# Reversed filter rows through a DRAM scratch and adding transfers: one change to a two-headed kernel (local attention beside a long convolution)

## The chip, the cores and the metric

The kernel runs on one core of a Trainium2 chip. A core has TensorE (PE in the profile, with PEld for its weight loads), VectorE (DVE), ScalarE (ACT), GpSimd (POOL) and SyncE (SP, which here only issues transfers), and 16 DMA engines that all queues share. The metric is the device time of one launch in microseconds, smaller is better: the median of several executions. Beside it stands one execution taken by the profiler, from which every duration below comes.

## The reference

Two independent computations stand side by side in the output (2048 rows, 576 columns each). Everything is bf16 in and out.

```
A: qkv = x @ wqkv; 32 heads of 18; each position attends to 8 positions, 2 apart
   logits = sum(q * k_gathered) * 18**-0.5; softmax over 8; o = sum(attn * v_gathered)
   a = o @ wo
B: k_shift = sum over 4 taps of k shifted by t, times shift_k;  kv = k_shift * v
   kv_f = rfft2(kv padded to (4096, 576));  kf_f = rfft2(ssm_k padded to 4096)
   y = irfft2(kv_f * kf_f)[:2048]  +  kv * ssm_D;   b = q * y
out = concat(a, b)
```

B is a causal convolution of kv with the filter ssm_k along the sequence, channel by channel; adding ssm_D to the filter's first tap gives the second term.

## The kernel before

**Part B** cuts the sequence into four blocks of 512. Each block of the filter (m = 0 to 3) and of kv (i = 0 to 3) is turned into a spectrum of 512 odd frequencies by matmuls against tables of cosines and sines (`filter_spectrum`, units "fk" and the block's number; `x_spectrum`, units "fx"). Output block j is the sum over i of the product of spectrum i of kv with spectrum j - i of the filter (`products`, on DVE, for three column groups t), summed by matmuls against an identity (`sums`, `sum_of`), turned back by matmuls (`inverse`, units "inv") and multiplied by q. A complex product is made with three real ones, so every spectrum has a third part, the sum of the first two: either an addition on DVE (`add_third`, or in `produce`) or, by `third`, a copy on SP's queue and an adding transfer on POOL's. Of the homes that receive products there are two for j = 0 and four for later j; DVE waits for PE before it writes one again.

A filter block stands in SBUF with 512 taps as four chunks of 128 partitions (`kTok`). The table is symmetric, so tap n and tap 512 - n can first be added and subtracted ("folded"), and the matmuls then need half the rows. For this the rows of the first two chunks have to be reversed. `fold_filter` does it on PE: for each half, matmuls against a reversing matrix, one that handles a single first row, and an identity, into PSUM (`ps_rev`), 12 matmuls for blocks 3 and 2 and 8 for blocks 1 and 0, two ACT evacuations, then three adding transfers on POOL. Before that, POOL copies one chunk of each block to a second place (`other`), SP moves the first rows of blocks 0 and 1 in a chain of six small copies (`first_rows`), and DVE negates a row of each block (`negate`).

**Part A** is projected by matmuls (units "proj" and "v", 8 to 18 matmuls each with one evacuation for two units), the logits are products on DVE that PE sums over a head's 18 columns (`logits`, `ps_log`), softmax is spread over DVE, ACT and PE, and the weighted sum over v is again products on DVE and sums on PE (`weigh`, `ps_acc`), then `output` (units "wo").

**The order** is written out by hand. DVE's work runs through the program in a fixed order: the taps (blocks 0 to 3), ten products of `logits(0)`, ten of `logits(1)` with softmax between, then `weigh` with n from 1 to 26, then `products`. PE's pieces that DVE does not wait for at once stand in one queue, `units`. At each call of `until()` the next number in `PLACES` says how many pieces are taken from its front and issued. The first four numbers belong to the taps, the fifth stands ahead of the logits, the next five behind every second product of `logits(0)`, then softmax and `logits(1)`, and so on. `need(label)` takes from the front until no piece with that label is left. `FKS` and `FXS` mix the spectra with the v projections; `EARLY` puts the first fk3 pieces between the last two mirrors (pieces labelled "x" that fold kv); `ZMIX`, `PRE`, `REGROUP` and `AT` place steps of the products, adds of thirds, the regrouping of v's weights, and the mirrors. Every engine works through its own list in order and waits by semaphores, so a piece that isn't ready stops those behind it on its engine.

**Queues.** SP issues the loads, the four transposing loads of the filter (`load_filter`), then `first_rows`, then much later the spreading of the attention weights and the copies of `third`. POOL issues all adding transfers and some loads (`load_q`, which fetch q for part B into `TB`).

Of the kernel before, what the change touches and what calls it, by code (L numbers as in the profile page):

```python
# [19 lines left out]
    2, 1, 1, 0, 1, 4,  # L20
# [3 lines left out]
    25, 22,  # L24
)

THIRDS = ((0, 1),), ((0, 2), (1, 2)), ((0, 3), (1, 3))

REGROUP = (
    15, 14,  # L30
# [3 lines left out]
    2, 14, 13, 4, 3, 0, 2, 4, 8, 2, 10, 2, 6, 1, 4, 4, 3, 6, 1, 3, 0, 5, 5, 5, 3, 3, 4, 2, 1, 0, 3, 11, 2, 2, 3,  # L34
    1, 1, 4, 0, 10, 0, 3, 0, 2, 11, 1, 1, 0,
# [10 lines left out]
    0, 0, 2,  # L46
# [3 lines left out]
    1, 5, 19,  # L50
# [9 lines left out]
def kernel(  # L60
# [40 lines left out]
    GORD = [0, 2, 1, 3]  # L101
    HD = 288
# [163 lines left out]
    flip1 = main.tile([128, 128], BF16, name="flip1")  # L266
    flip0 = main.tile([128, 128], BF16, name="flip0")
    corner = main.tile([128, 128], BF16, name="corner")
    corner2 = main.tile([128, 128], BF16, name="corner2")
    flip2r = main.tile([128, 128], BF16, name="flip2r")  # L270
    identn0 = main.tile([128, 128], BF16, name="identn0")
# [28 lines left out]
    nc.gpsimd.affine_select(flip1[:], ones128[:], pattern=[[1, 128]], compare_op=ALU.is_equal, fill=0.0,  # L300
                            base=-128, channel_multiplier=1)
    nc.gpsimd.tensor_copy(flip0[:], flip1[:])
    nc.gpsimd.tensor_copy(flip2r[:], flip1[:])
    nc.gpsimd.memset(flip1[0:1, 0:1], 1.0)
    nc.gpsimd.memset(flip2r[0:1, 0:1], 2.0 ** 0.5)
    nc.gpsimd.memset(corner[:], 0.0)
    nc.gpsimd.memset(corner2[:], 0.0)
    nc.gpsimd.memset(corner2[0:1, 0:1], 2.0 ** 0.5)
    nc.gpsimd.memset(corner[0:1, 0:1], 1.0)
    nc.gpsimd.tensor_copy(identn0[:], identn[:])  # L310
    nc.gpsimd.memset(identn0[0:1, 0:1], 0.0)
    nc.gpsimd.tensor_scalar(ident2[:], ident[:], 2.0, None, op0=ALU.mult)
# [241 lines left out]
    def with_sine(f, n):  # L554
        f()
        sines[n]()
        if n == 1:
            nc.gpsimd.memset(TK[0:1, 0, 1, :], 0.5)
            for gi, sg in enumerate((1, -1, -1, 1)):
                nc.gpsimd.memset(TK[0:1, 0, 0, 128 * gi:128 * gi + 128], sg * 0.5)  # L560
# [69 lines left out]
    logits_run = [False]  # L630

# [6 lines left out]
    def first_rows():  # L638
        nc.gpsimd.dma_start(row(0, 0), B_ssm_D.unsqueeze(0), accum_op=ALU.add)
# [8 lines left out]

    def spare(m):
        return view(Ks, k_at(1, 0) + D * m, [[1, D]])[0:1]  # L650

    signed = set()

    def negate(*ms):
# [691 lines left out]
```

## Time and profile before

| | us |
|---|---|
| median of 3 executions | 212.2 (212.09 to 212.56) |
| profiled execution | 212.5 |
| its span in the trace | 210.8 |

In the profile a line of a timeline gives start, duration, engine, source line, operation, output <- input, how many were merged, and in brackets the idle time before it with what ended that. Groups give a total and the mean of one in ns. Matmuls overlap in PE's pipeline, so for their cost the chain of waits (which counts each once) is the better row. The granted clock of PE is at 1.00 in nearly all of the span.

### The profile page before, as it was taken

How to read it: one execution, taken by the hardware profiler on the slowest of the kernel's cores; microseconds unless marked ns; L12 is line 12 of the kernel's file. 1: busy time of each engine (PE TensorE's matmuls, PEld its weight loads, DVE VectorE, ACT ScalarE, POOL GpSimd, SP SyncE). 2: the span in 40 equal slices, each digit the busy share in tenths (PEclk: the TensorE clock that was granted, in tenths of full speed). 3: DMA queues.
4: the chain of work that ended last, by engine and by line, in shares of the span. 5: the costliest groups of instructions: out<-in, count | busy, mean ns of one | idle time of the engine just before them, and what ended most of it. 6: DMA issues, size and time to landing. Idle time of an engine off the chain costs nothing.

```text
span 210.8 us, 5106 instructions
## 1 busy us (share of the span) xinstructions
PE 200.1 (95%) x2114; PEld 110.7 (53%) x2122; DVE 193.1 (92%) x146; ACT 150.5 (71%) x218; POOL 74.0 (35%) x111
## 2 busy tenths in 40 slices
PE   7999999999999999899999999999989999999891
PEld 2443443344554656564354666656555666666460
DVE  7989999999999999858889999999999849999981
ACT  3799988657684989986369788855666796775540
POOL 8999993001195516320175000002029004033000
PEclk9999999999999999999999999999999999999999
DMA  6999998999639336999999997587559995985133
GB/s 201 303 328 231 266 342 280 170 192 182 151 75 122 48 40 87 180 181 171 235 225 238 194 234 159 105 208 185 153 223 255 239 322 110 214 243 182 28 113 111
DMA packets 35396, 39.66 MB, mean 188 GB/s; under 512 B 17619, under 2 KB 29007, under 8 KB 35374
## 3 DMA queue, kind: packets, MB, share of 16 engines
q1 hardware_dynamic: 26812, 24.88, 47.2%
q0 software_dynamic: 6096, 11.96, 30.4%
q10 hardware_dynamic: 2466, 2.51, 3.5%
q8 instruction: 16, 0.26, 0.5%
q14 instruction: 6, 0.05, 0.1%
HBM read 13.11 MB, written 4.72 MB: 85 GB/s over the span
## 4 chain that ended last, share of the span: by engine, by line
PE 80%; ACT 10%; DVE 5%; issue 2%; DVEq 0%; ACTq 0%
PE ps_proj L378 16%; PE ps_z L1126 9%; PE ps_wo L1029 8%; PE ps_acc L973 7%; PE ps_inv L1158 7%; PE ps_fx L776 6%; PE ps_log L847 4%; PE ps_proj L500 3%; PE ps_fk L627 3%; PE ps_proj L382 3%; PE ps_proj L389 3%; ACT Ks L695 3%; PE ps_rev L673 2%; PE ps_fk L628 1%; ACT qk L977 1%
## 5 line engine op out<-in xcount | busy, mean ns | idle before, releaser
L378 PE MATMUL ps_proj<-xw 128*128 128x512 bf16 x153 | 37.4, 380 | 0.6 <-issue 0.3
L832 DVE TENSOR_TENSOR av<-qk 128x4096 bf16<-128x4096 bf16 (+1 forms) x16 | 31.7, 2013 | 2.8 <-PE ps_log L847 2.8
L378 PEld LDWEIGHTS <-xw 128*128 128x128 bf16 x160 | 14.0, 97 | 20.5 <-issue 6.2
L1099 DVE TENSOR_TENSOR qk<-xw,Ks 128x2304 bf16<-128x2304 bf16 x14 | 18.5, 1355 | 2.5 <-PE ps_inv L1158 2.4
L1139 ACT ACTIVATE av<-ps_z 128x768 bf16<-128x768 f32 x20 | 15.3, 808 | 6.2 <-PE ps_z L1126 6.2
L414 ACT ACTIVATE qk<-ps_proj 128x1024 bf16<-128x1024 f32 x14 | 14.3, 1023 | 7.6 <-PE ps_proj L389 3.3
L695 ACT ACTIVATE Ks<-ps_fk 128x576 bf16<-128x576 f32 x32 | 18.6, 717 | 1.3 <-PE ps_fk L628 1.3
L577 DVE TENSOR_TENSOR tB<-kj,skb 128x4608 bf16<-128x4608 bf16 (+1 forms) x8 | 19.3, 2417 | 0.1
L778 ACT ACTIVATE xw<-ps_fx 128x576 bf16<-128x576 f32 x32 | 18.4, 666 | 0.0
L776 PE MATMUL ps_fx<-xw,TB 128*128 128x288 bf16 x128 | 18.0, 286 | 0.2
L1055 POOL DMA_DIRECT2D Ks<-Ks x3 | 3.7, 1218 | 41.1 <-PE ps_wo L1029 28.7
L1029 PE MATMUL ps_wo<-qk 128*128 128x288 bf16 x128 | 17.8, 287 | 0.0
L627 PE MATMUL ps_fk<-Ks,TB 128*128 128x384 bf16 x62 | 16.9, 326 | 0.8 <-ACT Ks L695 0.7
L414 ACT ACTIVATE v<-ps_proj 128x1024 bf16<-128x1024 f32 x9 | 9.3, 1029 | 9.3 <-PE ps_proj L378 4.3
L973 PE MATMUL ps_acc<-av,ident 64*64 64x512 bf16 x160 | 15.3, 377 | 0.0
L628 PE MATMUL ps_fk<-Ks,TB 128*128 128x192 bf16 x62 | 15.2, 245 | 0.0
L776 PEld LDWEIGHTS <-TB 128*128 128x128 bf16 x128 | 12.0, 97 | 6.0 <-issue 2.9
L1029 PEld LDWEIGHTS <-qk 128*128 128x128 bf16 x128 | 11.6, 98 | 5.6 <-issue 3.0
L1158 PE MATMUL ps_inv<-av,TI 128*128 128x288 bf16 (+1 forms) x96 | 13.6, 293 | 0.6 <-ACT av L1139 0.6
L1161 ACT ACTIVATE v<-ps_inv 128x576 bf16<-128x576 f32 (+1 forms) x14 | 9.5, 677 | 6.3 <-PE ps_inv L1158 6.3
L977 ACT ACTIVATE qk<-ps_acc 128x1024 bf16<-128x1024 f32 x8 | 8.2, 1024 | 8.0 <-PE ps_acc L973 8.0
L956 DVE TENSOR_TENSOR av<-Ks,v 128x4096 bf16<-128x4096 bf16 x6 | 13.6, 2286 | 0.2 <-PE ps_acc L973 0.2
(199 smaller groups left out, 471.3 us busy)
## 6 DMA issues: line engine op xcount, KB each, us to landing
Ks<-Ks POOLq DMA_DIRECT2D x9, 576.0 KB, 7.1
TB<-av SPq DMA_DIRECT2D x12, 256.0 KB, 5.5
kj<-in_B_k_dram SPq DMA_DIRECT2D x6, 504.0 KB, 6.1
vt<-in_B_v_dram SPq DMA_DIRECT2D x8, 288.0 KB, 5.2
Ks<-av SPq DMA_DIRECT2D x8, 256.0 KB, 5.5
Ks<-Ks SPq DMA_DIRECT2D x3, 576.0 KB, 6.1
Ks<-in_A_x_dram SPq DMA_DIRECT2D x2, 576.0 KB, 5.2
xw<-in_A_wqkv_dram SPq DMA_DIRECT2D x2, 576.0 KB, 5.9
```

The costliest lines, as they stand in the source:

```text
L378: nc.tensor.matmul(ps[:, jp, :], wq(kb, comp, 128 * ct, 128), xT(kb, 1024 * jj + 512 * jp, 512), **se)
L414: nc.scalar.activation(view(t, o + pad + 1024 * jj, [[512, 2], [1, 512]]), ps[:], ACT.Copy)
L577: dve(2304 * n, lambda: nc.vector.tensor_tensor(to, view(kj, row * D, [[D, n], [D, 4], [1, D]]), view(skb, row * D, [[D, n], [0, 4], [1, D ...
L627: nc.tensor.matmul(o[:, 0:2], w, rhs[:, 0:2], start=start, stop=stop)
L695: nc.scalar.activation(view(Ks, k_at(m, cs ^ (m & 1)) + 96 * gi, [[768, 3], [384, 2], [1, 96]]), acc3(ps), ACT.Copy, scale=(PSG, MSG)[cs][ ...
L776: nc.tensor.matmul(ps[:, pm, 0:HD], TX[:, 2 * pm + c, 128 * gi:128 * gi + 128], kv[:, 2 * c + pm, HD * h:HD * h + HD], start=(c == 0), sto ...
L832: return P, at, step, dve(1024 * nj, lambda: nc.vector.tensor_tensor(view(P, at, [[step, 4], [256, nj], [1, 256]]), view(t, o + 256 * hh, ...
L973: nc.tensor.matmul(acc[64 * o:64 * o + 64, h, :], ident[64 * h:64 * h + 64, 64 * h:64 * h + 64], view(P, 256 * u, [[2048, 2], [1, 256]])[6 ...
L1029: nc.tensor.matmul(ps[:, r, 0:HD], oT(hh, 2 * c + r, t)[:, o:o + 128], wo[:, t // 2, t % 2, HD * h:HD * h + HD], start=(t == 0 and h == 0) ...
L1099: r = dve(3 * QTR, lambda: nc.vector.tensor_tensor(pr, view(xw, HB * XG[i] + QTR * t, [[HB, 3], [1, QTR]]), view(Ks, k_at(j - i, 0) + QTR ...
L1126: nc.tensor.matmul(view(acc[r], 512 * h, [[192, 2], [96, 2], [1, 96]])[o:o + 64], w[64 * h:64 * h + 64, 64 * h:64 * h + 64], pr[64 * h:64 ...
L1158: nc.tensor.matmul(ps[:, c, 0:n], TI[:, sl, pm, 128 * c:128 * c + 128], Y(j, pm)[:, sl, c0:c0 + n], start=(pm == 0 and sl == 0), stop=(sl ...
```

## The change

The reversal of blocks 2, 1 and 0 leaves PE. `turn_rows` writes the first two chunks of such a block to a scratch in DRAM (`bounce`, 130 rows of two chunks) with the row order reversed, on SP's queue: two large writes and three single rows for each block, in place of `first_rows`. `fold_filter` then has ACT write the negated and scaled base (four activations: `other`, two chunks, one row), and four adding transfers on POOL's queue add the reversed rows from DRAM to all four chunks and to `other`, by half the partitions at a time. The signs and the weight of the first row come from per-partition scales (`keep`, `minus`) and from a table row set to `KAPPA` instead of 0.5. Block 3 is still reversed by matmuls; its `other` is now written by ACT. POOL's four copies and DVE's `negate` go.

The rest concerns order. Folds 2, 1 and 0 enter the queue at places 2, 5 and 9 (`FOLDS`); six fk3 pieces are early, now behind both mirrors. The third part of block 0 of both spectra is left to `produce`, in three pieces; block 1 of kv (at n = 21) takes the place of block 1 of the filter among the thirds by transfer. Thirds of block 2 are issued ahead of `load_q`. Products of output blocks 2 and 3 have six homes instead of four, a home still in use is passed over, and output pieces of the first half of the heads ("wo0") must be issued before. All tables of the order have new numbers.

```diff
 ZMIX = (
-    2, 1, 1, 0, 1, 4,
+    3, 1, 0, 0, 1, 5,
 PRE = (
-    25, 22,
+    27, 33,
-THIRDS = ((0, 1),), ((0, 2), (1, 2)), ((0, 3), (1, 3))
+THIRDS = ((0, 0), (0, 1), (1, 1)), ((0, 2), (1, 2)), ((0, 3), (1, 3))
+BY_DMA = (
+    37, 32, 21,
 REGROUP = (
-    15, 14,
+    0, 7,
 PLACES = (
-    2, 14, 13, 4, 3, 0, 2, 4, 8, 2, 10, 2, 6, 1, 4, 4, 3, 6, 1, 3, 0, 5, 5, 5, 3, 3, 4, 2, 1, 0, 3, 11, 2, 2, 3,
-    1, 1, 4, 0, 10, 0, 3, 0, 2, 11, 1, 1, 0,
+    6, 11, 13, 5, 1, 1, 3, 4, 11, 3, 9, 3, 3, 1, 2, 5, 3, 4, 0, 5, 0, 5, 5, 6, 2, 5, 4, 1, 2, 1, 2, 12, 2, 2, 3,
+    1, 0, 5, 1, 2, 0, 3, 1, 9, 12, 1, 1, 0, 2, 11, 0, 0,
 FKS = (
-    5, 1, 0, 0, 0, 0, 0, 0, 0, 0, 0, 0, 0, 0, 0, 3, 0, 0, 0, 0, 0, 0, 0, 0, 0, 0, 0, 0, 0, 0,
+    5, 1, 0, 0, 0, 0, 0, 0, 0, 0, 0, 0, 0, 0, 0, 0, 0, 0, 0, 2, 0, 0, 0, 0, 0, 1, 0, 0, 2, 0,
 FXS = (
-    0, 0, 15, 0, 8, 0, 0, 4, 0,
+    0, 1, 1, 25, 2, 0, 0, 0, 0,
+FOLDS = (
+    2, 5, 9,
 EARLY = (
-    0, 0, 2,
+    0, 0, 6,
 AT = (
-    1, 5, 19,
+    0, 8, 9,
...
+    bounce = [dram.tile([130, 2 * D], BF16, name=f"bounce{m}") for m in range(NBL)]
...
-    def first_rows():
-        nc.gpsimd.dma_start(row(0, 0), B_ssm_D.unsqueeze(0), accum_op=ALU.add)
-        for step in range(3):
-            for m in (1, 0):
-                nc.sync.dma_start(*((spare(m), row(m, 0)), (row(m, 0), row(m, 1)), (row(m, 1), spare(m)))[step])
...
+    def turn_rows(m):
+
+        kt, t = kTok(m), bounce[m]
+        for c in range(2):
+            nc.sync.dma_start(bass.AP(tensor=t.tensor, offset=t.offset + 64 * 2 * D + (1 - c) * D,
+                                      ap=[[65 * 2 * D, 2], [-2 * D, 64], [1, D]]), kt[:, c, :])
+        nc.sync.dma_start(bass.AP(tensor=t.tensor, offset=t.offset + 65 * 2 * D, ap=[[2 * D, 1], [1, 2 * D]]),
+                          kTok(m)[0:1, 0:2, :].rearrange("p c d -> p (c d)"))
+        for c in range(2):
+            nc.sync.dma_start(bass.AP(tensor=t.tensor, offset=t.offset + (1 - c) * D, ap=[[2 * D, 1], [1, D]]),
+                              kt[64:65, c, :])
...
         def unit():
...
+            t = bounce[m]
+            act = nc.scalar.activation
+            act(other(m), kt[:, 2, :], ACT.Copy, scale=keep[:])
+            act(kt[:, 0, :], kt[:, 2, :], ACT.Copy, scale=minus[:])
+            act(kt[:, 1, :], kt[:, 3, :], ACT.Copy, scale=-1.0)
+            act(row(m, 2), row(m, 2), ACT.Copy, scale=1.0 / KAPPA)
+            clk["A"] += 2.5
+            for h in range(2):
+                rows = t.offset + 65 * 2 * D * (1 - h)
+                p = slice(64 * h, 64 * h + 64)
+                nc.gpsimd.dma_start(view(Ks[p], k_at(m, 2), [[2 * D, 2], [1, 2 * D]]),
+                                    bass.AP(tensor=t.tensor, offset=rows, ap=[[2 * D, 64], [0, 2], [1, 2 * D]]),
+                                    accum_op=ALU.add, max_dma_last_dim=4 * D)
+                nc.gpsimd.dma_start(other(m)[p], bass.AP(tensor=t.tensor, offset=rows, ap=[[2 * D, 64], [1, D]]),
+                                    accum_op=ALU.add)
+
+        def by_matmuls():
...
-            for m in (3, 2, 1, 0):
-                nc.gpsimd.dma_start(other(m), kTok(m)[:, 2, :])
-            first_rows()
+            nc.gpsimd.dma_start(row(0, 0), B_ssm_D.unsqueeze(0), accum_op=ALU.add)
+            for m in (2, 1, 0):
+                turn_rows(m)
...
-            now, first = first[0] + [fold_filter(2)] + first[1] + mirrors[:1] + first[2] + mirrors[1:], list(now)
+            now, first = first[0] + mirrors[:1] + first[1] + mirrors[1:] + first[2], list(now)
...
+    for m, at in zip((2, 1, 0), FOLDS):
+        units.insert(min(at, [u[2] for u in units].index(f"fk{m}")), fold_filter(m))
...
-        npr[0] = npr[0] + 1 if t < 2 or j else 0
+        if j > 1:
+            homes += ((qk, 0), (qk, HB))
+        if j > 1:
+            need("wo0")
+        while homes[npr[0] % len(homes)] in busy.values():
+            npr[0] += 1
+        home = busy[j, t, i] = homes[npr[0] % len(homes)]
+        npr[0] += 1
...
+            if new and (j, t) == (NBL - 1, 2):
+                until()
...
-            for x, m in THIRDS[0]:
+        for at, (x, m) in zip(BY_DMA, THIRDS[0]):
+            if n == at:
                 third(x, m)
...
     outputs(1, 1)
+    for x, n in THIRDS[1]:
+        third(x, n)
     load_q(0)
     load_q(1)
-    for x, n in THIRDS[1]:
-        if x:
-            need(f"fx{n}")
-        third(x, n)
...
```

More of the change, by code (lines that the diff above doesn't have):

```diff
@@ L1077, in store_b @@
     def store_b(j, c0, n, src, h):
-        other = nc.scalar if j == NBL - 1 else nc.sync
+        end = j == NBL - 1
+        other = nc.scalar if end else nc.sync
         if h == 0:
```

86 lines of the change are left out of this document (38 added, 48 removed).

## The prediction

> **What bounds the kernel now.** First the page's head and busy times, then the table of stages:
>
> ```profile
> span 210.8 us, 5106 instructions
> ...
> PE 200.1 (95%) x2114; PEld 110.7 (53%) x2122; DVE 193.1 (92%) x146; ACT 150.5 (71%) x218; POOL 74.0 (35%) x111
> ...
> 50.00:60.00 10.00, 9.37 (x88) 5.37 (x86) 9.90 (x10) 7.56 (x13) 3.11 (x6) 1.00 0.67 152
> 60.00:70.00 10.00, 9.95 (x101) 4.74 (x98) 10.00 (x8) 6.46 (x11) 6.24 (x8) 1.00 0.68 91
> 70.00:80.00 10.00, 9.91 (x98) 5.85 (x91) 9.96 (x7) 9.07 (x16) 4.96 (x6) 1.00 0.35 47
> 80.00:90.00 10.00, 9.24 (x80) 5.75 (x82) 8.82 (x7) 10.00 (x17) 4.63 (x5) 1.00 0.90 146
> ...
> 160.00:170.00 10.00, 10.00 (x136) 6.34 (x135) 7.78 (x7) 7.98 (x13) 3.12 (x4) 1.00 1.07 259
> 170.00:180.00 10.00, 10.00 (x147) 6.76 (x145) 8.41 (x7) 7.65 (x13) 2.34 (x2) 1.00 0.76 211
> ...
> 190.00:200.00 10.00, 9.09 (x179) 5.81 (x168) 10.00 (x9) 5.57 (x8) 1.92 (x3) 1.00 0.34 100
> 200.00:211.00 11.00, 5.76 (x88) 3.67 (x80) 5.53 (x7) 2.60 (x4) 0.00 (x0) 0.95 0.38 107
> ```
>
> The columns are busy times of PE, PEld, DVE, ACT and POOL, then granted clock, DMA share and GB/s. PE is full nearly throughout. Its work is a queue of pieces that only has to be finished, so the end moves by the PE work taken out plus the PE idle time put in or removed. DVE is as full from 50 to 80 us. ACT is full from 80 to 90, where PE loses 0.76 us. In the tail (190 on) DVE is at 100% and PE loses 0.91 us to 200 and, up to its end at 206.2, 6.2 - 5.76 = 0.4 us more: 1.3 us.
>
> **PE work removed.** The chain of waits and the groups show a reversal:
>
> ```profile
> 68.38 0.98 PE ps_rev L673 x8
> ...
> L676 ACT ACTIVATE Ks<-ps_rev 128x576 bf16<-128x576 f32 x8 | 4.8, 648 | 2.1 <-PE ps_rev L673 2.1
> ...
> 71.13 4.47 ACT L695 ACTIVATE Ks<-ps_fk 128x576 bf16<-128x576 f32 x8
> ...
> 93.14 1.71 ACT L695 ACTIVATE Ks<-ps_fk 128x576 bf16<-128x576 f32 x3
> ```
>
> Eight matmuls take 0.98 us, 0.1225 each. Block 2 had 12, blocks 1 and 0 had 8 each; block 3 keeps its 12. So 28 x 0.1225 = **3.4 us of PE** go, and six activations with them.
>
> **ACT work added.** Each of the three folds now has four activations of 576 columns in place of two, and block 3's fold has two more: 12 + 2 - 6 = 8 more. No row has one from SBUF to SBUF of this size; the nearest are the evacuations above, 0.648 us alone and 4.47 / 8 = 0.56 us in a series. A one-row activation with 576 columns is taken at the same price; bounds 8 x 0.56 = 4.5 us and 8 x 0.648 = 5.2. I take 4.5, since they stand in series. ACT's idle time from 60 to 80 us is 3.54 + 0.93 = 4.5 us by the table above, so they just fit if they come early enough; if the cover is gone, up to 5.2 us come onto the ACT-bound stretch from 80 us. The queue count below pops fold 2, 1 and 0 at the logits' second, third and fourth pair, about 61 to 70 us, where that idle time lies. I take **0**, bounds 0 and +4.5.
>
> The Trainium skill, "ScalarE: Activation LUTs", section "What ACT_TABLE_LOAD costs", says that each [128,1] pointer operand adds about 93 ns; seven of the new activations have such a scale, an estimate of 0.65 us on top. No activation with a pointer as its scale is in the trace to test this.
>
> **The order of PE's queue, by hand.** Popping counts ahead of the first logits were 3, 0, 2, 4, 8, 2; now 1, 1, 3, 4, 11, 3. The queue began v24, v24, v00, v00, fx, fk3; now both mirrors are popped by the "x" label and the six early fk3 stay ahead of everything: fk3, fk3, fold2, fk3, fk3, fold1, fk3, fk3, v24, fold0, v24, fx, v00, v00, fk3, fx, fk3, then fk2. The rows that price it:
>
> ```profile
> 50.61 0.61 PE ps_fold L606 x8
> ...
> 55.01 0.41 PE L673 MATMUL ps_rev<-Ks,identn 128*128 128x288 bf16 x2
> ...
> 55.02 1.75 DVE L901 TENSOR_SCALAR xw<-Ks 128x1152 int32<-128x1152 int32 x2
> ...
> 56.70 4.47 DVE L832 TENSOR_TENSOR av<-qk 128x4096 bf16<-128x4096 bf16 x2
> ...
> 59.73 1.92 PE L382 MATMUL ps_proj<-xw 128*64 128x512 bf16 x16
> ...
> 62.89 1.05 PE L847 MATMUL ps_log<-av,E 128*32 128x512 bf16 x16
> ...
> 63.87 3.40 DVE L832 TENSOR_TENSOR av<-qk 128x4096 bf16<-128x4096 bf16 x2
> ```
>
> Before, PE had fold 2 and three v pieces ahead of the first logits and came late: products ready at 61.17, logits at 62.89. Now the second of L901's two copies (0.58 us) and two sign changes (0.43) are no longer ahead of the products, so they are ready at about 60.2. PE by then has only the mirrors and two fk3 and is done at about 59.6 (estimate: fold 3 ends at 55.3, its last row less the pipeline's overlap, mirrors two times 0.61, fk3 two times 0.5, and waits for their evacuations): idle 0.6. Second pair: products every 2.2 us, ready at 64.6; PE has two fk3 (1.0) and half the logits: idle 1.9. Third pair: two fk3 and a v piece against DVE until 68.0 (a half product, 3.40 less 2.2, and a whole one): idle 0.4. From the fourth pair (11 pieces, 6.7 us) PE is behind DVE again. Sum 2.9, less about 0.3 us of waits there before: **+2.6 us of PE idle**, bounds 0 (PE never ahead of DVE) and 4.0 (three gaps with no piece at all of v in them). So of the 3.4 us only 0.8 remain at the end of this stage; they show as pieces done earlier (v01 before fk0 ends), not as an earlier fk0.
>
> **The bounce.** Removed: four POOL copies, six small chained SP copies. Added: 15 SP writes to DRAM and, for each fold, four adding POOL transfers (2 x 288 KB and 2 x 72 KB). Rows:
>
> ```profile
> 53.41 13.67 SPq L642 DMA_DIRECT2D Ks<-Ks  x6
> ...
> 57.97 0.54 POOL L736 DMA_DIRECT2D xw<-Ks  x1 [4.40 <-DMA Ks<-in_B_ssm_k_dram]
> ...
> 63.33 2.86 POOL L427 MEMSET v<- 128x64 bf16 x1
> ...
> 70.64 1.24 POOL L678 DMA_DIRECT2D Ks<-Ks  x1 [4.40 <-ACT Ks L676]
> ...
> Ks<-Ks POOLq DMA_DIRECT2D x4, 288.0 KB, 4.3
> ...
> out_dram<-TB SPq DMA_DIRECT2D x6, 144.0 KB, 4.0
> ```
>
> The writes for block 2 issue behind the transposes, at 53.4 on SP's queue, 0.5 to 0.6 us each, five a block: 56.2, plus 4.0 to land (the nearest write to DRAM): 60.5. Fold 2's activations overwrite what was sent, about 61, just after; blocks 1 and 0 follow at some 63.5 and 67.5 (block 0 also waits for the row added behind the transpose at 57.97, 2 us), against folds at 65 and 69. ACT is in order: a late write would stop everything behind it, mirrors' and logits' evacuations too. Behind the 15 writes on SP's queue stands only the small v pad copy, then nothing until the attention weights are spread, behind fk0. The adds: POOL's memsets of the v pads end at 66 at the latest, fold 2's issue takes 2 x 0.75 + 2 x 0.55 = 2.6 us, landing at 72 (64 + 2.6 + 4.3 = 71, one more for twice the bytes). fk2 begins behind the fourth pair at about 73.7. Cost **0** with 2 us to spare; bounds 0 and +7 (the four landing one behind the other, 64 + 4 x 4.3 = 81).
>
> **DVE and the tail.** Rows:
>
> ```profile
> 160.58 1.30 POOL L1055 DMA_DIRECT2D Ks<-Ks  x1
> ...
> 161.34 1.78 POOL L1055 DMA_DIRECT2D xw<-xw  x1
> ...
> DMA to landing us min/median/max: 5.4/7.7/12.7
> ...
> 170.28 1.36 DVE L1099 TENSOR_TENSOR qk<-xw,Ks 128x2304 bf16<-128x2304 bf16 x1 [2.40 <-PE ps_inv L1158]
> ...
> 174.22 1.36 DVE L1099 TENSOR_TENSOR v<-xw,Ks 128x2304 bf16<-128x2304 bf16 x1 [1.30 <-PE ps_wo L1021]
> ...
> 136.06 1.19 ACT L778 ACTIVATE xw<-ps_fx 128x576 bf16<-128x576 f32 x2
> ...
> 195.93 0.36 PE L1126 MATMUL ps_z<-qk,ident 64*64 64x384 bf16 x4 [0.32 <-DVE qk L1099]
> ...
> 197.36 1.46 PE L1158 MATMUL ps_inv<-av,TI 128*128 128x384 bf16 x8 [0.58 <-ACT av L1139]
> ...
> 205.47 0.70 PE ps_back L1185 x14
> ...
> 156.74 0.74 POOL L1087 DMA_DIRECT2D TB<-in_B_q_dram  x1 [11.97 <-DVE qk L956]
> ```
>
> DVE's two waits are named PE, but the first products of output block 2 need the third parts that POOL's two adds write. 161.34 + 12.7, the longest landing, is 174.04, and DVE goes on at 174.22; 160.58 + 9.7 is 170.28. I read both as late adds: they stood behind the q loads, which waited until 156.74, and DMA was full (1.07 in the table). The change puts the adds ahead of these loads, and the j=0 sums run a step earlier. So up to 2.40 + 1.30 = 3.7 us of DVE waits go. Two more homes for products of blocks 2 and 3 let DVE use that lead; they cost no operation. DVE also loses work:
>
> ```profile
> L657 DVE TENSOR_SCALAR Ks<-Ks 1x576 bf16<-1x576 bf16 x3 | 0.8, 303 | 0.0
> ...
> L1062 DVE TENSOR_TENSOR Ks<-Ks 128x2304 bf16<-128x2304 bf16 x1 | 1.4, 1351 | 0.0
> ...
> L1244 DVE TENSOR_TENSOR Ks<-Ks 128x768 bf16<-128x768 bf16 x2 | 1.1, 554 | 0.0
> ```
>
> Four sign changes go (about 1.0 us); of the j=0 thirds, two whole adds (2 x 1.35) become three pieces (3 x 0.55): 1.05 us less. BY_DMA 37 and 32 are never reached by a loop that ends at 26, so only block 1 of the input goes by DMA (n = 21) where block 1 of the filter did: one 1.35 us add for another, and its transfer has from 137 us, when the last fx is evacuated, to 159. DVE thus comes to its last product 3.7 + 2 us sooner if PE lets it, and most of PE's 1.3 us of tail idle goes; half of the 0.58 us before L1158 is kept, since there PE waits for ACT to copy the sums: **-1.0 us**, bounds 0 and -1.3. Should the adds be late still, the product loop keeps today's tail.
>
> **Sum.** -3.4 + 2.6 + 0 + 0 - 1.0 = -1.8 us. The profiled execution took 212.5 us, 1.7 around its span of 210.8, and stands 0.3 above the median 212.2: 212.5 - 1.8 = 210.7, and 0.3 less against the median: **210.4**.
>
> **Rivals.** (a) ACT decides, slower: the folds' activations stand in front of the fk evacuations, and the time from 69 us to fk0's last evacuation becomes ACT's alone. For it: ACT is at 10.00 from 80 to 90 already, and 4.5 us come to an idle time of 4.5, part of which it cannot use (waits for logits and writes). It decides from about 1.8 us of overflow on; with all 4.5 overflowing, PE loses them and keeps 0.8 + 1.0: 212.2 + 2.7 = 214.9; with half, 212.2 + 0.5 = 212.7. Against: six fk3 and both first folds come before 68. (b) The bounce is late: fk2 waits up to 7 us at 73.7, 212.2 + 7 - 1.8 = 217.4, or 2.5 us of it, 212.9. Against: consecutive adds of the before trace overlap. (c) PE is never ahead of DVE (mirrors or fold 3 later than I place them): no idle of 2.6, 212.2 - 3.4 - 1.0 = 207.8. For it: PE was 1.7 us late at the first logits; against: it has four pieces fewer before them now. (d) All is given back: gaps of 4 us and the third adds late as now: 212.2 - 3.4 + 4.0 = 212.8, and 212.2 with gaps of 3.4: the reversal is off PE, but PE idles instead. For it: DVE is at 10.00 from 60 to 80, so PE cannot run ahead of the logits; against: the adds are issued earlier.
>
> **Numbers.** Forecast (208.9 to 211.7) 0.47; (c) 0.17; (a) 0.18; (b) 0.08; (d) 0.10. A difference of over 0.2% is what can be told here. Faster: 0.47 + 0.17 and a little = 0.65; same 0.07, from (d); slower 0.28. Range: 207.8, the whole of (c), to 213.2, the milder halves of (a), (b) and (d).
>
> **What will show it.** Right: no ps_rev matmul after 57 us; PE gaps of 0.5 to 2 us ahead of the logits between 58 and 68; ACT without gaps from 69 to about 95; no DVE wait of over 1 us between 165 and 176; PE full after 190. Wrong: the first fk2 waiting for a DMA, ACT waiting for a write to the bounce, the last fk0 evacuated after 96.5 us (it ends at 94.85 now), or DVE still waiting at the first products of block 2.

## The result, and the profile after

The changed kernel took 226.9 us (median of four; three took 225.7 to 227.1) against 212.2 for the kernel before: ratio 1.067, with an interval of 1.063 to 1.070. The other one took 494.8 us, which the record does not explain, and ratios here and below leave out executions over 1.5% above a kernel's fastest. It is **14.7 us slower**; the prediction said 1.8 us faster, and 226.9 lies far outside its range. The profiled execution took 227.1 us, with a span of 225.3.

The page's head and the table of stages of the changed kernel (columns as in the prediction: length, busy time of PE, PEld, DVE, ACT, POOL, then granted clock, DMA share, GB/s):

```profile
span 225.3 us, 5046 instructions
...
PE 203.0 (90%) x2084; PEld 112.0 (50%) x2094; DVE 191.4 (85%) x143; ACT 156.7 (70%) x226; POOL 71.3 (32%) x105
```

```profile
60.00:70.00 10.00, 7.79 (x66) 3.40 (x64) 9.11 (x6) 9.38 (x16) 5.46 (x10) 0.84 0.63 111
70.00:80.00 10.00, 6.60 (x47) 2.30 (x45) 5.92 (x3) 1.80 (x3) 3.27 (x4) 0.84 0.74 130
80.00:90.00 10.00, 5.29 (x24) 3.10 (x23) 0.00 (x0) 6.97 (x11) 3.71 (x4) 0.52 0.48 73
```

Between 70 and 90 us first ACT and then DVE stands still: ACT does 1.8 us of work in one slice, DVE none in the next, and PE idles for 8.1 us of the two. The timelines of the changed kernel say who waits for whom. First ACT, then PE, then DVE (start, duration, engine, line, operation; in brackets the idle time before it and what ended it):

```profile
81.52 0.78 ACT L667 ACTIVATE Ks<-Ks,minus 128x576 bf16<-128x576 bf16 x1 [7.83 <-DMA bounce<-Ks]
```

```profile
84.39 0.48 PE L635 MATMUL ps_fk<-Ks,TB 128*128 128x384 bf16 x1 [7.74 <-ACT v L424]
```

```profile
74.21 2.29 DVE L846 TENSOR_TENSOR v<-qk 128x4096 bf16<-128x4096 bf16 x1
90.61 3.43 DVE L846 TENSOR_TENSOR av<-qk 128x2048 bf16<-128x2048 bf16 x2 [14.11 <-PE ps_log L861]
94.86 0.21 DVE L889 TENSOR_TENSOR av<-av,maskb 32x128 bf16<-32x128 bf16 x1 [0.83 <-ACT av L866]
```

The head of the whole queue is one activation of fold 0 (L667). It overwrites filter rows that the write to the DRAM scratch still has to read. It waits 7.83 us for that write; the evacuations behind it in ACT's list wait too, so PE's results stay in PSUM, the logits come late, and DVE waits 14.11 us. The addition of the mask row (line L889, L875 before) is the first step of the first softmax. It came at 79.34 before and at 94.86 now: 15.5 us later, while the end is 14.5 us later. So **the whole loss lies ahead of the mask row**.

The chain of waits of the changed kernel (start, duration, what) leads back to SP's queue, and SP's timeline shows the 15 writes being issued:

```profile
62.07 5.30 SPq L654
67.42 13.99 DMA bounce<-Ks
81.52 0.11 ACT Ks L667
```

```profile
49.22 1.20 SPq L652 DMA_DIRECT2D bounce<-Ks  x2
...
52.26 3.05 SPq L652 DMA_DIRECT2D bounce<-Ks  x2
55.36 3.48 SPq L654 DMA_DIRECT2D bounce<-Ks  x1
...
59.53 2.50 SPq L652 DMA_DIRECT2D bounce<-Ks  x2
62.07 5.30 SPq L654 DMA_DIRECT2D bounce<-Ks  x1
67.42 0.54 SPq L657 DMA_DIRECT2D bounce<-Ks  x2
```

Block 2's writes are issued in 0.5 to 1.2 us each. From block 1 on an issue takes up to 5.30 us; I read that as a queue that is full ahead of it. The last write lands at 81.5. The six big writes are 6 x 144 KB = 885 KB; from 49.2 to 81.5 that is 32.3 us, 27 GB/s on average. The view of the DMA queues (queue, packets, MB, share of all 16 engines; q1 carries what SP issues, q0 what POOL issues) says more. First the writes from 55 to 60 us, where little else moves, then both queues from 77 to 80:

```profile
q1 hardware_dynamic: 190, 0.21, 12.6%
```

```profile
q0 software_dynamic: 33, 0.05, 9.4%
q1 hardware_dynamic: 34, 0.04, 4.4%
```

A share of 12.6% is 2.0 of 16 engines; 0.21 MB in 5 us are 42 GB/s, 21 for each engine. From 77 to 80 the writes get only 4.4% and 13 GB/s, and both queues together hold 2.2 engines. That fits adding transfers of the folds that share the two engines with the writes, but the profile doesn't name the engine of a packet, so this is argued. At 42 GB/s throughout, the 885 KB would end near 70 (an estimate from these rows), before L667 wants them: by it the long wait needs both, the two engines and the adds on them.

The access pattern of these writes on the DRAM side is two runs of 64 rows, stepping backwards: its outermost size is 2. Theory 1 is therefore that **the outermost size of the pattern sets the number of engines**. The Trainium skill has this as a rule ("DMA: Bandwidth & Descriptors", section "Why a DMA increments its semaphore by 16 and not by 1"): the largest k up to 16 that divides the slowest dimension of both sides. By that rule k is 2 here; the runs below agree with it, with 2.0 engines at 2 and 4.1 at 4. At 16 they show 7.8 on average, which is more than at 4 but no count of 16.

### The profile page after: what moved, and what is told of

Read it like the earlier page. It is cut to its first block, busy times and chain, and to the rows that moved or that the text cites. A ratio compares the mean times of both kernels' runs of the same rounds, so it can differ in the third digit from the quotient of the medians.

```text
span 225.3 us, 5046 instructions
## 1 busy us (share of the span) xinstructions
PE 203.0 (90%) x2084; PEld 112.0 (50%) x2094; DVE 191.4 (85%) x143; ACT 156.7 (70%) x226; POOL 71.3 (32%) x105
## 4 chain that ended last, share of the span: by engine, by line
PE 67%; SPq 11%; ACT 10%; DMA 6%; issue 2%; DVE 1%; ACTq 0%; DVEq 0%
PE ps_proj L388 12%; PE ps_z L1151 8%; PE ps_inv L1183 7%; PE ps_acc L987 7%; DMA bounce<-Ks 6%; PE ps_wo L1043 6%; PE ps_fx L790 6%; SPq L654 4%; PE ps_proj L510 3%; PE ps_fk L635 3%; SPq L652 3%; SPq L240 3%; PE ps_log L861 3%; PE ps_proj L399 2%; ACT av L1164 1%
## 5 line engine op out<-in xcount | busy, mean ns | idle before, releaser
L635 PE MATMUL ps_fk<-Ks,TB 128*128 128x384 bf16 x62 | 19.4, 364 | 9.7 <-ACT v L424 7.7
L1123 DVE TENSOR_TENSOR qk<-xw,Ks 128x2304 bf16<-128x2304 bf16 x16 | 21.1, 1353 | 0.0
L636 PE MATMUL ps_fk<-Ks,TB 128*128 128x192 bf16 x62 | 16.5, 267 | 0.0
L790 PEld LDWEIGHTS <-TB 128*128 128x128 bf16 x128 | 12.1, 99 | 7.3 <-issue 4.2
L970 DVE TENSOR_TENSOR av<-Ks,v 128x4096 bf16<-128x4096 bf16 x6 | 13.7, 2287 | 1.2 <-PE ps_acc L987 1.2
L1070 POOL DMA_DIRECT2D xw<-xw x3 | 3.6, 1198 | 32.0 <-ACT TB L1050 30.5
L1183 PEld LDWEIGHTS <-TI 128*128 128x128 bf16 x112 | 10.5, 98 | 5.6 <-issue 2.7
```

Source lines behind the costliest of these rows:

```text
L635: nc.tensor.matmul(o[:, 0:2], w, rhs[:, 0:2], start=start, stop=stop)
L790: nc.tensor.matmul(ps[:, pm, 0:HD], TX[:, 2 * pm + c, 128 * gi:128 * gi + 128], kv[:, 2 * c + pm, HD * h:HD * h + HD], start=(c == 0), sto ...
L1123: r = dve(3 * QTR, lambda: nc.vector.tensor_tensor(pr, view(xw, HB * XG[i] + QTR * t, [[HB, 3], [1, QTR]]), view(Ks, k_at(j - i, 0) + QTR ...
L1183: nc.tensor.matmul(ps[:, c, 0:n], TI[:, sl, pm, 128 * c:128 * c + 128], Y(j, pm)[:, sl, c0:c0 + n], start=(pm == 0 and sl == 0), stop=(sl ...
```

## The experiments

All times are medians; each ratio is against runs of the kernel before on the same chip (212.2 to 212.3 us in every group).

**1. The writes: engines, direction, queue.** Three kernels change only how the scratch is written. blocks16 and blocks4 reverse rows within blocks of 8 or 32, forward2 steps forwards. All three thereby compute with another filter; they are there for their times.

```diff
-  ap=[[65 * 2 * D, 2], [-2 * D, 64], [1, D]]     # changed kernel
+  ap=[[8 * 2 * D, 16], [-2 * D, 8], [1, D]]      # blocks16
+  ap=[[32 * 2 * D, 4], [-2 * D, 32], [1, D]]     # blocks4
+  ap=[[65 * 2 * D, 2], [2 * D, 64], [1, D]]      # forward2
```

> The changed kernel with the same bytes written to the scratch, the same rows of 1152 B and the same backward steps, but the slowest dimension of the DRAM side counts 16 (blocks of 8 rows, reversed within a block) instead of 2. The scratch's rows stand in another order, so the folded filter is another one. Theory 1 (a write whose slowest dimension counts 2 runs on 2 of the 16 DMA engines, and the six big writes go through these two in turn until 81.5 us): the writes issue at about 0.6 us each, all have landed by 66 us, ACT's wait of 7.8 us at fold 0 and the 5.3 us issue on SP are gone, and the time falls by 12 to 16 us, to 211 to 215. Theory 2 (backward steps, or DRAM as the target, are slow in themselves): as slow as the changed kernel, 225 to 228. Theory 3 (the order of the pieces and the ACT load are at fault, and the wait only shows where it ends): at most 4 us of the loss go, 222 or more.

> The changed kernel with the scratch's rows written forward in the two halves, the slowest dimension still counting 2; the rows are not reversed, so the folded filter is another one. Theory 1 (two engines): no better than the changed kernel, 225 to 228, with ACT waiting 7 to 8 us at fold 0. Theory 2 (backward steps are slow): the wait goes, 211 to 215.

> The changed kernel with the scratch rows written in 4 blocks of 32, reversed inside each block: the slowest dimension is 4 instead of 2 or 16, the rest as in blocks16 (the filter's rows come in another order). Theory 1 (the number of engines is the slowest dimension, at 13.7 GB/s each as in the changed kernel): 885 KB at 4 x 13.7 = 55 GB/s take 16 us, so the last write of SP's queue is issued at about 59 to 62 and lands by about 68; no wait of ACT for a write above 1 us, and 214.3 to 216. Rival (16 blocks are fast for another reason, such as the place of the rows in memory, and anything less is served like 2): the issue of SP's third single-row write stays at 62 or later and takes over 4 us, ACT waits over 5 us, 222 or more.

blocks16: 214.8 us (1.0114, 1.0085 to 1.0144). forward2: 227.1 (1.0705, 1.0677 to 1.0733). blocks4: 214.2 (1.0092, 1.0074 to 1.0110). The waits of ACT in forward2 hold the same line as in the changed kernel:

```profile
ACT Ks L667 <- DMA bounce<-Ks: 8.0, 1, 8.0
```

In blocks16 and blocks4 there is no such line. The issue that took 5.30 us, and SP's queue in the DMA view, first of blocks16 (52 to 56 us), then of blocks4 (52 to 58):

```profile
57.40 0.43 SPq L654 DMA_DIRECT2D bounce<-Ks  x1
...
q1 hardware_dynamic: 530, 0.54, 48.9%
```

```profile
58.86 0.47 SPq L654 DMA_DIRECT2D bounce<-Ks  x1
...
q1 hardware_dynamic: 471, 0.52, 25.7%
```

The issue that took 5.30 us takes 0.43 and 0.47. With an outermost size of 4 the writes hold 25.7%, 4.1 engines of 16, and move 87 GB/s, twice the changed kernel's 42. (The expectation of blocks4 used 13.7 GB/s an engine, half the average of 27; the rate without other traffic is 21.) Four engines do as well here as more: blocks4 is no slower than blocks16. Backward steps cost nothing (forward2); the size of the outermost dimension is the cause. It is worth 226.9 - 214.8 = **12.1 of the 14.7 us** by the medians, 11.7 by the ratios.

**2. The same writes from POOL's queue.** All of `turn_rows` is issued by `nc.gpsimd` in place of `nc.sync`.

> The changed kernel with the writes to the scratch issued from POOL's queue instead of SP's, access patterns unchanged. Theory 1, if POOL's transfers of this shape are dealt out over changing engines: the six writes overlap, land by about 65 us, and the time falls to 211 to 216. If POOL's are held to the same two engines, or if the target is the slow part: 224 to 228. POOL is blocked ahead by the transposing loads, so fold 3's adds may come 2 to 3 us later than now; that would show as fk3 waiting for a transfer.

222.9 us (1.049, 1.0448 to 1.0533), between the two ranges of the expectation. ACT waits only 0.7 us for a write, for from this queue the writes overlap, a median of 7.7 us each to land, and adds run beside the last of them only. But the adds of block 3's fold stand behind them on POOL's queue and are issued at 67.10 instead of 58.79 (blocks16). PE's timeline in pool_bounce:

```profile
73.38 0.50 PE L635 MATMUL ps_fk<-Ks,TB 128*128 128x384 bf16 x1 [8.28 <-DMA Ks<-Ks]
```

A wait is exchanged for another one of the same size.

**3. Can the order hide the slow writes?** Four kernels keep the writes in their two-engine form: fold_late moves the folds back in PE's queue, late_even also spreads the pieces, fold0_mm takes block 0 out of the scratch (matmuls again), split sends block 0's writes through POOL.

```diff
-FOLDS = (2, 5, 9)
+FOLDS = (3, 13, 27)                 # fold_late, late_even; fold0_mm has (2, 5, 10)
-PLACES = (6, 11, 13, 5, 1, 1, 3, 4, 11, 3, ...
+PLACES = (6, 11, 13, 5, 1, 2, 4, 6, 7, 3, ...   # late_even
-        if m == NBL - 1:
+        if m in (0, NBL - 1):       # fold0_mm
-            for m in (2, 1, 0): turn_rows(m)
+            turn_rows(2); turn_rows(1)   # split; turn_rows(0, nc.gpsimd) after fold 3's adds, FOLDS (2, 7, 14)
```

> The changed kernel with its writes as they are (six big ones in the two-engine form), but the folds stand later in the queue of pieces: at 3, 13 and 27 instead of 2, 5 and 9, so that fold 0 is popped at about 80, when the last write has landed (81.5 in the changed kernel). Theory 1 (the whole of the big loss is ScalarE standing behind a write that is not there yet): the wait of ACT for a write is under 1.5 us, and the time falls to 212.5 to 215. Rival (the writes cost as transfers, by what they take from the others, or the adds then come too late for the spectra of block 0): PE waits over 3 us for a transfer at the spectra of block 0 or 1, and the time stays above 218.

> fold_late with the pieces ahead of the first logits spread evenly: counts 1, 2, 4, 6, 7, 3 instead of 1, 1, 3, 4, 11, 3. Theory P (what is left besides ScalarE's work is the 11 pieces ahead of the fourth pair of logits, for which VectorE's last two half products wait): that wait (3.10 us in blocks16) falls under 1 us, and the time is 1 to 2 us below fold_late. Rival (ScalarE is full, so that pieces popped earlier only wait for their evacuations): the wait moves to the second or third pair and the time stays within 0.5 us of fold_late.

> The changed kernel, but block 0 is reversed by matmuls as block 3 is (12 matmuls, 4 activations): only four of the six big writes to the scratch are left, 590 KB in the same form. At the 27.4 GB/s of the changed kernel they take 21.5 us from 49.2, so the last lands at about 71, before or at the fold that needs it. Theory 1 (the writes' two engines make the loss): no wait of ACT for a write above 2 us, 213.5 to 216.5. Rival (the first activation of a fold is delayed by something else than the amount written): ACT still waits over 5 us and the time stays above 222.

> The changed kernel with the writes divided: blocks 2 and 1 on SP's queue as now, block 0 on POOL's behind the adds of block 3, and the folds at 2, 7 and 14 in the queue. Theory 1 (two engines serve the writes of SP's queue, others those of POOL's, as pool_bounce showed, and the loss is ScalarE behind a write): ACT's wait for a write falls under 2 us, the spectra wait under 3 us for adds, and the time comes near blocks16, 214 to 218. Rival (any write in this form is late for some fold or some add, as in fold_late): a wait of over 5 us for a transfer stays on ACT or PE and the time stays above 220.

fold_late: 232.0 us (1.0939, 1.0893 to 1.0986), late_even: 234.4 (230.7 to 234.8), both slower than the changed kernel; between the two nothing can be told. The waits of PE in fold_late:

```profile
PE ps_fk L635 <- DMA Ks<-bounce: 7.8, 1, 7.8
PE ps_fk L635 <- DMA Ks<-Ks: 2.7, 2, 2.1
```

ACT no longer waits for a write, but fold 0 now comes at 91, and its adds take until 103 while the spectra of block 0 want them at 95. The folds count as pieces, so moving them back also puts other pieces ahead of the logits: DVE waits 6.4 us for the fourth pair, and the mask row comes at 88.6. A fold has two limits: it comes after its write has landed, and some 8 us before the first spectrum of its block. fold_late missed the second; in split fold 0 stands at 80, and PE doesn't wait for its adds. fold0_mm: 219.0 (1.0284, 1.0226 to 1.0341), above theory 1's range. split: 219.7 by the median, 217.6 by its ratio (1.0251, 1.0203 to 1.0299), at the upper end of theory 1's range at best. In fold0_mm's profile (220.3 us) ACT still waits 2.1 us for block 1's write, and the 12 matmuls of block 0 stand ahead of the fourth pair of logits, for which DVE waits 8.4 us. In split's (220.9 us) ACT waits for no write; PE waits 3.4 us for block 3's adds, and DVE 6.9 us for the same logits. No order that was tried makes up for the two engines.

**4. What is left: 2.6 us.** blocks16 has fast writes and 28 matmuls less on PE, and is still slower than before. Its PE and DVE timelines:

```profile
59.07 1.22 PE L614 MATMUL ps_fold<-xw,fold 128*64 128x288 bf16 x8 [2.48 <-ACT xw L617]
...
65.20 0.61 PE L861 MATMUL ps_log<-av,E 128*32 128x512 bf16 x8 [0.39 <-DVE av L846]
...
70.00 0.62 PE L861 MATMUL ps_log<-v,E 128*32 128x512 bf16 x8 [1.57 <-ACT Ks L711]
```

```profile
78.76 3.43 DVE L846 TENSOR_TENSOR av<-qk 128x2048 bf16<-128x2048 bf16 x2 [3.10 <-PE ps_log L861]
83.01 0.21 DVE L889 TENSOR_TENSOR av<-av,maskb 32x128 bf16<-32x128 bf16 x1 [0.83 <-ACT av L866]
```

noact2 is blocks16 without ten activations (per fold the two sign changes and the row scale; block 3's row scale). late3 moves block 3's two added activations and its adds behind the second mirror. noact_even is noact2 with the pieces spread as in late_even.

```diff
-            act(kt[:, 0, :], kt[:, 2, :], ACT.Copy, scale=minus[:])     # noact2, noact_even
-            act(kt[:, 1, :], kt[:, 3, :], ACT.Copy, scale=-1.0)
-            act(row(m, 2), row(m, 2), ACT.Copy, scale=1.0 / KAPPA)
-now, first = first[0] + mirrors[:1] + first[1] + mirrors[1:] + first[2], list(now)
+now, first = first[0] + mirrors[:1] + first[1] + mirrors[1:] + late3 + first[2], list(now)   # late3
```

> blocks16 without ten of ScalarE's activations: each of the three folds keeps only the copy into the other half (the two sign changes and the row scale are left out), and block 3's fold keeps its copy but not its row scale. By the rows of the changed kernel that is 3 x (0.76 + 0.67 + 0.67) + 0.68 = 7.0 us off ACT between 55 and 80 us. blocks16 took 214.8, 2.6 above before. Theory A (ScalarE's added work is what is left of the loss: it overflows its idle time and the filter spectra wait): 212.0 or less, ACT idle again from 60 to 80, the first softmax mask row within 1.5 us of 79.3 (83.0 in blocks16). Theory B (PE idles ahead of logits that VectorE paces, in the new order of the queue, whatever ACT does): 214.3 to 215, and the same gaps of PE between 58 and 71.

> blocks16, but block 3's two added activations (0.79 + 0.68 us) and its adding transfers come after the second mirror instead of inside block 3's fold. Theory A2 (the second mirror's wait of 2.48 us for ACT's copy of the first costs the end): that wait falls to about 1.0, and the time by 1 to 1.5 us, to 213.3 to 213.8. Theory B (PE then only waits longer at the first logits, which VectorE's products pace): the wait before the mirror shrinks, one before the first logits matmuls grows by as much, and the time stays 214.5 to 215.2.

> noact2 (blocks16 without ten of ScalarE's activations; 213.0 us) with the same even counts 1, 2, 4, 6, 7, 3. There VectorE still waits 1.60 us for the fourth pair of logits. Theory P: that wait goes, the first softmax mask row comes at 79.3 to 79.8 (80.93 in noact2), and the time falls to 211.4 to 212.0. Rival (VectorE's pace alone sets it): 212.7 to 213.2 as before.

noact2: 213.0 us (1.0036, 1.0023 to 1.0049). It is 1.8 us below blocks16, so leaving out ten activations, two more than the change adds, gives back 1.8 of the 2.6. Theory A asked for 212.0 and was missed by 1.0, theory B for 214.3 or more. DVE in noact2:

```profile
76.67 3.43 DVE L842 TENSOR_TENSOR av<-qk 128x2048 bf16<-128x2048 bf16 x2 [1.60 <-PE ps_log L857]
80.93 0.21 DVE L885 TENSOR_TENSOR av<-av,maskb 32x128 bf16<-32x128 bf16 x1 [0.83 <-ACT av L862]
```

The wait for the fourth pair of logits is 1.60 instead of 3.10, and the mask row comes 2.1 us earlier. late3: 214.2 us (1.0089, 1.0072 to 1.0105), not to be told from blocks16; it lies between the two ranges. The mirror waits 1.2 us instead of 2.5, and in PE's waits in late3 the one ahead of the logits has grown from 0.4 us to 1.3:

```profile
PE ps_log L865 <- DVE av L850: 1.3, 1, 1.3
...
PE ps_fold L614 <- ACT xw L617: 1.2, 1, 1.2
```

Most of the wait moved, as theory B had it. noact_even: 213.3 us (1.0045, 1.0029 to 1.0061), no gain: DVE's 1.60 became 0.33 and 1.34, and the mask row stays at 81.1. Theory P falls.

**5. What is PE's time worth ahead of the mask row?** norev is the kernel before without the reversed terms of blocks 2, 1 and 0: 16 of the matmuls go, nothing takes their place. norev_pull also moves three pieces ahead of the fourth pair of logits.

```diff
+                turns = turns if m == NBL - 1 else turns[-1:]         # norev, norev_pull
-    2, 14, 13, 4, 3, 0, 2, 4, 8, 2, 10, ...
+    2, 14, 13, 4, 3, 0, 2, 4, 11, 2, 7, ...                          # norev_pull
```

> The kernel before, with the reversed terms of blocks 2, 1 and 0 left out and nothing in their place: each of these folds keeps the four matmuls that copy the second column pair, and its activations, adds and sign changes; 16 matmuls of 0.1225 us go, 2.0 us of PE between 55 and 76 us. My prediction's step (PE is full nearly throughout, so work taken off it ends the kernel earlier, less what it then idles): 0.8 of 3.4 there, at least 0.5 us here, 211.0 to 211.8. Theory W (in that stretch VectorE is at 10.00 and paces the logits, so that PE work taken out turns into idle in full; the first softmax mask row stays at 79.1 to 79.5): 212.0 to 212.4.

> norev, with three pieces more ahead of the fourth pair of logits and three fewer after the fifth (counts 11, 2, 7 in place of 8, 2, 10), so that PE has later work to do in the time set free. Theory W: what PE's freed time is worth shows only when later pieces are pulled into it; the mask row stays by 79.8 and the time falls by about the three pieces, 1.0 to 1.6 us, to 210.6 to 211.3. Rival (ScalarE, 9.07 and 10.00 from 70 to 90, has to evacuate these pieces, so the pull only moves the wait): within 0.4 us of norev.

norev: 211.8 us (0.9959, 0.9940 to 0.9979): 2.0 us of PE work taken out bring 0.5 by the medians, 0.9 by the ratio. The time is within what my step gave, outside theory W; but the place is theory W's. DVE's timeline in norev:

```profile
75.99 3.41 DVE L833 TENSOR_TENSOR av<-qk 128x2048 bf16<-128x2048 bf16 x2
79.33 0.21 DVE L876 TENSOR_TENSOR av<-av,maskb 32x128 bf16<-32x128 bf16 x1
```

The mask row stands at 79.33 (79.34 before): DVE runs without a gap, and PE cannot make it earlier. I read the gain as pieces that PE finished ahead of the mask row and need not do behind it. norev_pull: 212.5 us (1.0008, 0.9995 to 1.0021), 0.7 slower than norev. With 11 pieces ahead of the fourth pair in place of 8 the logits come later, DVE waits 1.26 us for that pair, and the mask row comes at 81.00.

**6. The tail.** thirds_first and before_mix put parts of the change into the kernel before: thirds of block 2 ahead of the loads of q; pieces for block 0's thirds, six homes and the thirds between the two loads. pieces has block 0's thirds in pieces alone. b16_q_first is blocks16 with the thirds behind the loads, as before.

```diff
     outputs(1, 1)
-    load_q(0)
-    load_q(1)
     for x, n in THIRDS[1]:
         ...
         third(x, n)
+    load_q(0)
+    load_q(1)          # thirds_first; b16_q_first is the reverse; before_mix puts only load_q(1) behind
-PRE = (25, 22)
+PRE = (27, 27)         # pieces, before_mix: the loop takes block 0 in pieces
```

> The kernel before with one edit: the thirds of block 2 are issued ahead of the loads of q. My step: DVE's waits of 2.40 and 1.30 us at the first products of output block 2 are POOL's adds landing late behind the q loads; both fall below 0.5 us, DVE's last product ends about 3 us earlier, and of PE's 1.3 us of idle in the tail about 1.0 go: 211.0 to 211.6. Rival: the waits are for PE to free the homes, as the profile names them: they stay, and so does the time, 212.0 to 212.4.

> blocks16, but the third parts of block 2 are added after the loads of q, as in the kernel before. Theory T (my step for the tail: late adds hold VectorE at the first products of output block 2): waits of 2.4 and 1.3 us come back at these products and the time rises by 0.7 to 1.3 us, to 215.5 to 216.1. Rival (VectorE's later waits eat what it gains there, as in thirds_first): the waits come back and the time stays within 0.4 us of 214.8.

> The kernel before, with one part of the change alone: the thirds of block 0 are added by VectorE in pieces (0.55 us each) instead of two whole adds of 1.35 us, 1.05 us less for VectorE after 135 us. In every run so far the time from the first mask row to the end of the span was 130.2 to 130.5 us with the change and 131.5 without. Theory V (VectorE's 1.05 us set that difference): 211.0 to 211.5. Rival (the other homes, or PE's lighter queue, set it): 212.0 to 212.5.

> The kernel before with the three parts of the change that touch only the tail: thirds of block 0 added in pieces, six homes for products of blocks 2 and 3, and the third parts of block 2 added between the two loads of q. Theory V: VectorE comes 1.05 us earlier and waits less at the first products of block 2, 210.9 to 211.6. Rival (the tail is set by PE's queue and the transfers of block 3's thirds, as thirds_first and pieces showed): 212.0 to 213.2.

thirds_first: 213.1 us, 212.1 to 215.6 (1.0022, 0.9995 to 1.0048). b16_q_first: 214.4 (1.0103, 1.0080 to 1.0126), not to be told from blocks16. pieces: 212.3 (1.0000, 0.9989 to 1.0010). before_mix: 214.0 (1.0075, 1.0048 to 1.0102). DVE's waits of over 0.5 us after 165 us, first in b16_q_first, then in blocks16 (the last one, 0.78 in both, is left out):

```profile
175.52 1.36 DVE L1123 TENSOR_TENSOR qk<-xw,Ks 128x2304 bf16<-128x2304 bf16 x1 [1.83 <-DMA xw<-xw]
...
205.12 0.96 DVE L1162 CAST av<-ps_z 128x768 bf16<-128x768 f32 x1 [1.60 <-PE ps_z L1151]
```

```profile
185.56 1.36 DVE L1237 TENSOR_TENSOR TB<-v,TB 128x2304 bf16<-128x2304 bf16 x1 [0.95 <-ACT v L1231]
...
205.89 0.96 DVE L1162 CAST av<-ps_z 128x768 bf16<-128x768 f32 x1 [2.48 <-PE ps_z L1151]
```

In b16_q_first a wait of 1.83 us comes back at the first products of block 2 and costs nothing: without it, in blocks16, DVE waits just as long later, 0.95 + 2.48 = 3.43 us in all against 1.83 + 1.60 = 3.43. before_mix, whose parts were to gain 1 us, costs 1.7, outside both ranges: DVE waits 3.47 us for PE ahead of a product of block 0 or 1, and later 2.38 us for an add. Its timeline in before_mix:

```profile
161.49 1.36 DVE L1107 TENSOR_TENSOR Ks<-xw,Ks 128x2304 bf16<-128x2304 bf16 x1 [3.47 <-PE ps_z L1135]
...
185.65 1.36 DVE L1107 TENSOR_TENSOR v<-xw,Ks 128x2304 bf16<-128x2304 bf16 x1 [2.38 <-DMA Ks<-Ks]
```

## Why the prediction was wrong

The mask row divides the span, and the two parts can be read apart (rows of DVE's line with `maskb`, and the span):

| kernel | time (median) | profiled span | mask row | span less mask row |
|---|---|---|---|---|
| before | 212.2 | 210.8 | 79.34 | 131.5 |
| changed | 226.9 | 225.3 | 94.86 | 130.4 |
| blocks16 | 214.8 | 213.5 | 83.01 | 130.5 |
| blocks4 | 214.2 | 212.4 | 81.9 | 130.5 |
| noact2 | 213.0 | 211.4 | 80.93 | 130.5 |
| b16_q_first | 214.4 | 212.7 | 82.2 | 130.5 |
| norev | 211.8 | 210.0 | 79.33 | 130.7 |

**The bounce (predicted 0, bounds 0 and +7): +12.1.** This is the step that failed: "0.5 to 0.6 us each, five a block: 56.2, plus 4.0 to land (the nearest write to DRAM)". The row from which the 4.0 us came is the store of the output, of the same 144 KB, but the outermost size of its pattern is 128 (line L1080). The write is not a matter of bytes: with an outermost size of 2 it runs on two engines at 42 GB/s and, once the folds' adds run, at less; the six stand one behind the other, so the last landed at 81.5 and not at 67.5. That the adds would slow the writes had no term in the sum at all. The bound of 7 was also made from the wrong transfer, the adds; the mechanism it should have priced, ACT's queue standing behind a late write, was named in the same paragraph and given no size. The list of signs had it ("ACT waiting for a write to the bounce"), and rival (b) put the lateness at the spectra, with 0.08.

**ACT (predicted 0, bounds 0 and +4.5): about +1.8.** A term that was mis-sized, near rival (a). The eight activations fit the idle time of 4.5 us only on paper: a fold's four take 0.77, 0.76, 0.67 and 0.67 us, 2.6 us in a row since they overlap a little, not 4 x 0.56 = 2.24, and they stand ahead of the evacuations of mirrors and spectra that PE needs at once. Rows of the changed kernel:

```profile
62.94 0.77 ACT L666 ACTIVATE Ks<-Ks,keep 128x576 bf16<-128x576 bf16 x1
63.61 0.76 ACT L667 ACTIVATE Ks<-Ks,minus 128x576 bf16<-128x576 bf16 x1
64.28 0.67 ACT L668 ACTIVATE Ks<-Ks 128x576 bf16<-128x576 bf16 x1
64.85 0.67 ACT L669 ACTIVATE Ks<-Ks 1x576 bf16<-1x576 bf16 x1
```

Those with a pointer as scale take 0.09 to 0.10 us more than the one with a constant. The Trainium skill ("ScalarE: Activation LUTs", "What ACT_TABLE_LOAD costs") gives about 93 ns for it; the trace agrees. The one-row activation costs as much as the one with 128 rows.

**PE's work and its idle time (predicted -3.4 + 2.6 = -0.8): about -1.0 behind the mask row.** The 28 matmuls went, and behind the mask row every kernel of the table that has the change is 1.0 us shorter than before, whatever the thirds do (b16_q_first). norev has 0.8 of that from 16 matmuls alone. That the rest is of the same kind is argued, not shown. The number is near, but the mechanism is another than the one forecast: the end does not move by PE's work less its idle time. DVE, at 10.00 from 60 to 80, sets the mask row, so taking out PE work ahead of it cannot bring it forward (norev), while PE work that delays its logits moves it back (norev_pull). The gaps of PE came about where they were forecast, not in those sizes, as PE's timeline in noact2 shows:

```profile
57.87 0.98 PE L614 MATMUL ps_fold<-xw,fold 128*64 128x288 bf16 x8 [1.80 <-ACT xw L617]
...
62.38 0.62 PE L857 MATMUL ps_log<-v,E 128*32 128x512 bf16 x8 [0.39 <-DVE v L842]
64.59 0.61 PE L857 MATMUL ps_log<-av,E 128*32 128x512 bf16 x8 [1.59 <-DVE av L842]
```

PE waits 1.80 us at the second mirror, which the prediction had at 0.6 ahead of the first logits, and 0.39 and 1.59 at later ones, forecast at 1.9 and 0.4: 3.8 in all against 2.9, so that the total is near by luck. And the prediction left a wait the other way round without a price: "From the fourth pair (11 pieces, 6.7 us) PE is behind DVE again". There DVE waits 1.60 us for PE in noact2 and 3.10 in blocks16.

**The tail (predicted -1.0): nothing.** The reading of the waits as late adds is borne out for one of the two: in blocks16 DVE has no wait of over 1 us at these products, and with the adds behind the loads of q one of 1.83 us, for an add, comes back. (The match "160.58 + 9.7 is 170.28" showed nothing: 9.7 is in no row, it was taken from the time that it had to explain.) But the wait was not on the path. With it (b16_q_first) the time is the same, and in the kernel before the same edits gain nothing (thirds_first, pieces) or lose 1.7 us (before_mix). The time that DVE gained is waited away elsewhere.

**The sum by the runs:** -1.0 behind the mask row and, ahead of it, +12.1 for the writes, +1.8 for ACT, and what is left, 14.7 + 1.0 - 12.1 - 1.8 = +1.8. noact2 still shows 1.6 of these at the mask row (80.93 against 79.34): DVE's wait of 1.60 for the fourth pair. norev_pull has a wait of this kind, and a mask row as late, from 11 pieces ahead of that pair alone. Spreading the pieces did not remove it, but noact_even has as many pieces up to that pair (1 + 2 + 4 + 6 + 7) as noact2 (1 + 1 + 3 + 4 + 11), 20 with the folds; the kernel before has 17 (3 + 0 + 2 + 4 + 8). Fewer of them ahead of the pair was not tried with the change, so what would remove the wait is open. Also not tried is a correct reversal in a pattern that more than two engines serve.

No version that computes the reference beat the kernel before.

## What to carry to other kernels

Price a transfer by its access pattern, not by its bytes: look at the outermost size on both sides first, and take the price from a row with the same one. Before an in-place update follows a store of the same data, work out what stands behind it on its engine if the store is late, and give that a number. And look for the engine that paces a stage before counting work off another one: with DVE at 10.00 ahead of the mask row, 2.0 us of matmuls were worth 0.5 to 0.9.

## What the hardware showed that was not expected

- **Issue time shows a slow queue.** With two engines behind it, one issue on SP's queue took 5.30 us in place of 0.43; the queue's own timeline shows the backlog 20 us before anything waits for it.
- **The same pattern takes more engines from POOL's queue, at little more speed.** There the writes overlapped: POOL's queue held 25.3% from 55 to 60 in pool_bounce, four engines, but moved 0.25 MB against 0.21 from SP's queue. ACT's wait fell from 7.8 to 0.7 us; as block 3's adds stand behind the writes there, it is open how much of that is the queue's.
- **A stall of PE is paid twice.** During the 7.7 us wait of the changed kernel the granted clock fell to 0.50; the matmuls behind it took 0.52 us instead of 0.33 until about 89.5. The slice of the stall and matmuls behind it:

```profile
80.00:84.39 4.39, 0.00 (x0) 0.00 (x0) 0.00 (x0) 2.87 (x5) 0.66 (x2) 0.50 0.03 8
```

```profile
86.74 0.52 PE L635 MATMUL ps_fk<-Ks,TB 128*128 128x384 bf16 x1
```

Behind shorter waits at the mirror it fell too, but not always: the clock was 0.81 from 60 to 65 in blocks16 after 2.48 us and 0.74 in noact_even after 1.81, and 1.00 in noact2 after 1.80.
